# The product of two weights in a fused attention and two-MLP kernel: formed first in native float32 and kept in DRAM, instead of in the last block of the first MLP

## Chip, cores, metric

One core of one Trainium2 chip. The metric is the device time of one execution in microseconds; the kernel before takes 963.7 us (median of 3 runs).

## What is computed

```python
# attention: a recurrence over 768 steps, 4 batches x 8 heads of width 48
for t in range(S):
    S_re, S_im = ar*S_re - ai*S_im + k[t] v[t]^T, ar*S_im + ai*S_re
    y[t] = q[t] @ S_re
x = y as 3072 tokens x 384
# first MLP, d_ff = 2048
h = x @ w_in
g = max(h, 0) + log1p(exp(-abs(h)))
x = g @ w_out
# second MLP, d_ff = 1024; no nonlinearity between w3 and w_out
a = x @ w1;  b = x @ w2
h = a * b @ w3
return h @ w_out
```

The weights of both MLPs lie in DRAM as float64, which the kernel sees as pairs of int32 and turns into float32 itself.

## The kernel before

Tokens are 24 units of 128. Attention works unit by unit: a scan on DVE (`cmul`, tiles P and tm), a store and a transposing reload through DRAM (pd and rs), score matmuls (sc), DVE's mask (am), the matmuls yp, small DMAs that reorder y, and a copy to x. The first MLP (stage A) goes over nine blocks of tokens: 128, 256, then seven of 384. For each of 16 slices f of w_in and w_out (16 tiles of 128x768), `s1` multiplies by w_in and forms the softplus on ACT and DVE, and `s2a` adds the slice's share to three accumulators (acc); attention for later blocks is interleaved. The second MLP (stage B, `s3` and `s2b`) goes over six blocks of 512.

The first two blocks use native float32 matmuls with the weights w32; from the third on, weights and activations are split into a high and a low part of type float32r and multiplied in three products, each of which takes one pass.

Because nothing lies between w3 and the last w_out, the kernel forms their product W' (1024x384, tiles bwp) once and uses it in stage B. Before, this happens in the last block of stage A, in which no attention is left: `wo2_load` (L903) loads and converts eight pieces of w_out with three DVE operations (`to_f32`) and splits them; `w3_piece` (L913) does the same with 24 pieces of w3 transposed and issues three float32r matmuls per piece and column group into the PSUM tiles wpa; the last piece of a group splits the sums straight into bwp. `w12_conv` (L936) converts w1 and w2 in the same block. The loop at L949 sets when each is called.

wio (w_in and w_out of the first MLP) is converted in another, shorter way: `w_load` (L765) loads each half piece shifted by one int16, so that ACT's copy of bf16 to f16 (`wtop`) and one DVE operation give the float32 (`w_piece`, L774). These loads start at the beginning and go into eight buffers wb0 to wb7; the converted w32 lie in wa0 to wa15.

The order of all instructions is not the program's: `Plan` records every operation with a cost and a landing time from a table (`cost`, L128), simulates the engines (`run`, `flush`) and emits the best order found in 16 rounds. Every recorded operation therefore has one line in the profile, L200. SP issues all DMAs, in the planned order.

Of the kernel before, what the change touches and what calls it, by code (L numbers as in the profile page):

```python
# [11 lines left out]
F32 = mybir.dt.float32  # L12
F32R = mybir.dt.float32r
# [42 lines left out]
CV0 = 20  # L56
CVS = 10
LEAD = 0
ROUNDS = 16
SEED = 214  # L60
NBA = NT // NB
# [15 lines left out]
class Plan:  # L77
# [50 lines left out]
    def cost(self, eng, op, outs, ins):  # L128
        n = max(self.free_size(x) for x in (*outs, *ins))
        if eng == "SP":  # L130
            size = 2 if outs[0].dtype == I16 else 4
            for _, n in outs[0].ap:
                size *= n
            cost = max(650 if n < 512 and self.on_chip(ins[0]) else 475, size / 270)
            if not self.on_chip(outs[0]):
                land = 5200
            elif self.on_chip(ins[0]):
                land = 2300
            elif hasattr(ins[0].tensor, "tag_meta"):
                land = 6800  # L140
            else:
                land = 2500 + size / 270
            return cost, max(land - cost, 0)
        if eng == "PE":
            n = self.free_size(outs[0])
            if op == "transpose":
                return 109, 250
            m = outs[0].ap[0][1]
            if ins[0].dtype == F32R:
                return n / 2.4 + 14, 250  # L150
            return (0.75 * n + 24 if m <= 64 else max(n, m) / 0.6 + 5), 250
        if eng == "DVE":
            far = [x for x in ins if x.ap[-1][0] >= 4 and x.ap[-1][1] > 1]
            return 72 + n / (1.92 if op == "tensor_scalar" else 0.52 if len(far) > 1 else 0.95), 200
        if eng == "ACT":
            return 105 + 0.88 * n, 200
        return 160 + n * 2.08, 200
# [198 lines left out]
def fused(ctx: ExitStack, tc: tile.TileContext, a_in, qk_in, v_in, wio, w12, w3t, wo2, q, k, v, a_re, a_im, outT):  # L356
# [67 lines left out]
    def load(u):  # L424
        s = c[u]
        if u in (2, 3):
            t = sp.tile([P, KC, NB], F32, tag="xl", bufs=XB, name=f"a{u}")
            s["a"] = t.rearrange("p k n -> p (k n)")[:, 0 : 2 * GT].rearrange("p (c n) -> p c n", c=2)
        else:
            s["a"] = ap.tile([P, 2, GT], F32, tag="n2" if u == 1 else "a", bufs=1, name=f"a{u}")  # L430
        SP.dma_start(s["a"], a_in[u])
# [311 lines left out]
    def split(dst_h, dst_l, src):  # L743
        A.copy(dst_h, src)
        V.tensor_tensor(out=dst_l, in0=src, in1=dst_h.bitcast(F32), op=ALU.subtract)

    def to_f32(dst, raw):
        lo, hi, d = raw[:, :, 0], raw[:, :, 1], dst.bitcast(I32)
        V.tensor_scalar(
            out=d, in0=hi, scalar1=3, scalar2=0x3FFFFFF8, op0=ALU.logical_shift_left, op1=ALU.bitwise_and  # L750
        )
        V.scalar_tensor_tensor(
            out=d, in0=hi, scalar=-0x40000000, in1=d, op0=ALU.bitwise_and, op1=ALU.bitwise_or
        )
        V.scalar_tensor_tensor(
            out=d, in0=lo, scalar=29, in1=d, op0=ALU.logical_shift_right, op1=ALU.bitwise_or
        )
# [4 lines left out]
    for x in wtop:  # L762
        GP.memset(x, 0)

    def w_load(f):  # L765
        r = wraw[f] = wp.tile([P, 2 * DM, 2], I32, tag=f"wb{f % (FA // 2)}", name=f"wr{f}")
        n = 4 * DM
        for i in range(2):
            SP.dma_start(
                r.rearrange("p n w -> p (n w)").bitcast(I16)[:, i * n : (i + 1) * n - i],  # L770
                wio[f].bitcast(I16)[:, i * n + 1 : (i + 1) * n + 1 - i],
            )

    def w_piece(f):  # L774
        w32[f] = wp.tile([P, 2 * DM], F32, tag=f"wa{f}", name=f"w32_{f}")
        r, top = wraw.pop(f), wtop[f % 2 if f < FA - 1 else 0]
        A.copy(
            top.bitcast(F16).rearrange("p (n w) -> p n w", w=2)[:, :, 1],
            r.rearrange("p n w -> p (n w)").bitcast(BF16).rearrange("p (n w) -> p n w", w=4)[:, :, 2],
        )  # L780
        V.scalar_tensor_tensor(
            out=w32[f].bitcast(I32), in0=r[:, :, 0], scalar=13, in1=top, op0=ALU.logical_shift_right, op1=ALU.bitwise_or
        )

    whp = {}

# [78 lines left out]
            SP.dma_start(dst(i), o[:, 0:n])  # L865

    load(0)
    for f in range(4):
        w_load(f)
    first = att_end[BLOCKS[0][1] // T - 1]  # L870
# [6 lines left out]
    bwp = [None] * (FB // 2)  # L877
    bst = {}

    nraw, nwt, nw3 = count(), count(), count()  # L880

    def wt(name):
        tag, n = (("n2", 2 * DM), ("tm", 4 * TML))[next(nwt) % 2]
        return ap.tile([P, n], F32, tag=tag, name=name)[:, 0 : 2 * DM]

    def w3t_pair(name):
        i = next(nw3) % 3
        if i == 0:
            t = ap.tile([P, H * (64 + D)], F32R, tag="kT", name=name)
            return t[:, 0:DM], t[:, DM : 2 * DM]  # L890
        tags = ((("am", AMB, 4 * T), ("y", YB, 4 * T)), (("S", 2, DM),) * 2)[i - 1]
        return tuple(
            ap.tile([P, n], F32R, tag=tag, bufs=bufs, name=f"{name}_{j}")[:, 0:DM]
            for j, (tag, bufs, n) in enumerate(tags)
        )

    def raw3(src, n, name):
        tag, bufs = (("a", 1), ("qk", QB), ("nt", NTB))[next(nraw) % 3]
        r = ap.tile([P, DM, 2], I32, tag=tag, bufs=bufs, name=name)
        SP.dma_start(r[:, 0:n], src.rearrange("p (n w) -> p n w", w=2))  # L900
        return r[:, 0:n]

    def wo2_load(k):  # L903
        t = wt(f"wo2t{k}")[:, 0:DM]
        to_f32(t, raw3(wo2[k], DM, f"wo2r{k}"))
        if k % 2 == 0:
            tag, bufs, n = (("P", PB, 2 * R * GT), ("P", PB, 2 * R * GT), ("qkp", QKB, 4 * DM), ("rs0", 1, 2 * H * T))[k // 2]
            oo = ap.tile([P, n], F32R, tag=tag, bufs=bufs, name=f"wo2_{k}")
            bst["oo"] = oo[:, 0 : 4 * DM].rearrange("p (a b n) -> p a b n", a=2, b=2)
        o = bst["o", k] = bst["oo"][:, k % 2]  # L910
        split(o[:, 0], o[:, 1], t)

    def w3_piece(m0, n, k):  # L913
        t = wt(f"w3t{m0}_{k}")[:, 0 : n * P]
        to_f32(t, raw3(w3t[k, :, 2 * m0 * P : 2 * (m0 + n) * P], n * P, f"w3r{m0}_{k}"))
        w = w3t_pair(f"w3_{m0}_{k}")
        split(w[0][:, 0 : n * P], w[1][:, 0 : n * P], t)
        if k == 0:
            for i in range(n):
                bst["a", i] = pst(ATAG, ATT, [P, DM], f"wpa{m0 + i}")  # L920
        o = bst["o", k]
        for q, (a, b) in enumerate(((0, 0), (1, 0), (0, 1))):
            for i in range(n):
                PE.matmul(
                    bst["a", i], w[a][:, i * P : (i + 1) * P], o[:, b],
                    start=(k == 0 and q == 0), stop=(k == FB - 1 and q == 2),
                )
        if k == FB - 1:
            for i in range(n):
                m = m0 + i  # L930
                if m % 2 == 0:
                    bwp[m // 2] = w_tiles(m // 2, f"bwp{m // 2}")
                dh, dl = (x[:, (m % 2) * DM : (m % 2 + 1) * DM] for x in bwp[m // 2])
                split(dh, dl, bst["a", i])

    def w12_conv(j):  # L936
        t = wt(f"w12t{j}")
# [4 lines left out]
        split(bw[j][0], bw[j][1], t)  # L942

    nblk = len(BLOCKS)
    st = [lambda k=k: wo2_load(k) for k in range(FB)]
    for m0 in range(0, FB, 3):
        st += [lambda m0=m0, k=k: w3_piece(m0, min(3, FB - m0), k) for k in range(FB)]
    pos = 0
    for bi in range(nblk):  # L949
        last = bi == nblk - 1  # L950
        t0, n = BLOCKS[bi]
        if not last:
            start = att_pos[0]
            goal = att_end[sum(BLOCKS[bi + 1]) // T - 1] + LEAD
        gq = {}
        for f in range(FA):
            if bi == 0:
                if f + 4 < FA:
                    w_load(f + 4)
                if f + 2 < FA:  # L960
                    w_piece(f + 2)
            gq[f] = s1(bi, f)
            if f >= 2:
                s2a(bi, f - 2, gq.pop(f - 2))
            if not last:
                att_to(start + (goal - start) * (f + 1) // FA)
            elif f >= 2:
                while pos < len(st) * (f + 1) // FA:
                    st[pos]()
                    pos += 1  # L970
                if f >= 7 and f - 7 < FB - 2:
                    w12_conv(f - 7)
        for f in (FA - 2, FA - 1):
            s2a(bi, f, gq.pop(f))
        evac(n, lambda i: x2d[t0 // NB][:, i, t0 % NB : t0 % NB + n], f"a{bi}",
             lambda name: sp.tile([P, NB], F32, tag="e", name=name))
# [337 lines left out]
```

## Time and profile before

| | us |
|---|---|
| runs | 962.29, 963.7, 965.88 |
| median | 963.7 |
| the profiled execution's own time | 962.8 |
| its span | 961.0 |

The profile shows that one execution. Windows give the busy time of each engine in a stretch; a matmul's end is modelled, so neighbouring matmuls overlap, and the pace of PE is read from start to start. PEclk is the granted clock of TensorE as a share of full speed. The chain of waits is followed back from the last instruction.

### The profile page before, as it was taken

To read this page: it belongs to the slowest core of one execution; us is meant where nothing else is said; L and a number is where in the kernel's file an instruction comes from. 1 tells how busy PE (TensorE), PEld (TensorE's weight loads), DVE (VectorE), ACT (ScalarE), POOL (GpSimd) and SP (SyncE) were. 2 spreads that over 40 slices of the span, in tenths; PEclk is the share of its full clock that TensorE was granted. 3 is DMA by queue.
4 is the path that set the end of the run, shared out by engine and by line. 5 is a ranking of instruction groups with operands and counts; after the bars stand their busy time and mean duration, and the time that the engine had idled before them with its cause. 6 is when DMAs were issued, how large, how long until landed. Compare 5 with 4: busy or idle time off the path is not lost.

```text
span 961.0 us, 15859 instructions
## 1 busy us (share of the span) xinstructions
PE 876.4 (91%) x5737; PEld 807.5 (84%) x5737; DVE 769.4 (80%) x1707; ACT 539.3 (56%) x1108; POOL 6.8 (1%) x15
## 2 busy tenths in 40 slices
PE   0037899999999999999999999999999999999996
PEld 0027888899899999999999999998888888888885
DVE  7997999999998999999988787998978887422121
ACT  6766666686678786887775675564231322131221
POOL 2000000000000000000000000000000000000000
PEclk9997999999999999999999999999999999999998
DMA  8774563837365545446371844556877767100001
GB/s 322 293 178 127 124 158 85 196 92 142 98 143 128 126 111 134 118 101 180 87 158 64 194 161 154 165 156 189 247 244 244 258 200 243 45 33 1 34 0 37
DMA packets 87399, 138.61 MB, mean 144 GB/s; under 512 B 8080, under 2 KB 58384, under 8 KB 87312
## 3 DMA queue, kind: packets, MB, share of 16 engines
q1 hardware_dynamic: 87312, 137.52, 51.8%
q8 instruction: 46, 0.75, 0.4%
q14 instruction: 41, 0.34, 0.1%
HBM read 108.00 MB, written 28.31 MB: 142 GB/s over the span
## 4 chain that ended last, share of the span: by engine, by line
PE 80%; DVE 10%; DMA 6%; issue 1%; ACT 1%; SPq 1%; DVEq 0%; ACTq 0%
PE acc L200 29%; PE s L200 18%; PE pb L200 10%; PE pa L200 10%; PE wpa L200 3%; PE yp L200 3%; PE sc L200 3%; DVE P L200 3%; DMA a<-a_in 3%; DMA wr<-wio 2%; DVE tm L200 2%; PE stp L200 1%; DVE qkp L200 1%; SPq L200 1%; DMA rs<-pd 1%
## 5 line engine op out<-in xcount | busy, mean ns | idle before, releaser
L200 DVE TENSOR_TENSOR tm<-P 128x90 f32<-128x90 f32 (+3 forms) x240 | 145.8, 616 | 1.4
L200 ACT ACTIVATE e<-e 128x384 f32<-128x384 f32 (+2 forms) x288 | 135.4, 487 | 2.8
L200 DVE TENSOR_TENSOR bg<-pa,bg 128x512 f32<-128x512 f32 x48 | 33.0, 690 | 87.3 <-PE pa L200 70.9
L200 ACT ACTIVATE e<-s 128x384 f32<-128x384 f32 (+2 forms) x144 | 64.6, 452 | 48.5 <-PE s L200 40.1
L200 DVE TENSOR_TENSOR P<-tm 128x45 f32<-128x45 f32 (+11 forms) x304 | 86.1, 344 | 1.4
L200 DVE SCALAR_TENSOR_TENSOR g<-s,e 128x384 f32<-128x384 f32 (+2 forms) x144 | 73.8, 515 | 14.3 <-ACT e L200 12.0
L200 ACT CAST bgg<-bg 128x512 fp32r<-128x512 f32 x48 | 29.8, 621 | 98.1 <-DVE bg L200 98.1
L200 PE MATMUL ktp<-ident,qkp 128*128 128x128 f32 x120 | 21.4, 288 | 62.4 <-DVE qkp L200 60.2
L200 ACT COPY bg<-pb 128x512 f32<-128x512 f32 x48 | 28.2, 587 | 87.1 <-PE pb L200 87.1
L200 PEld LDWEIGHTS ktp<-ident,qkp 128*128 128x128 f32 x120 | 16.0, 149 | 63.8 <-issue 53.6
L200 ACT CAST gh<-g 128x384 fp32r<-128x384 f32 x112 | 56.6, 510 | 18.6 <-DVE g L200 16.2
L200 DVE TENSOR_TENSOR gl<-g,gh 128x384 fp32r<-128x384 f32 x112 | 62.2, 558 | 5.5 <-ACT gh L200 5.0
L200 PE MATMUL sc<-rs 112*128 112x128 f32 x384 | 56.7, 290 | 8.4 <-DMA rs<-pd 7.2
L200 PEld LDWEIGHTS sc<-rs 112*128 112x128 f32 x384 | 54.4, 204 | 9.5 <-issue 7.8
L200 DVE CUSTOM_DVE_ANT_0 ck<-ckr 128x384 f32<-128x384 f32 x80 | 43.4, 543 | 14.2 <-DMA ckr<-w3t 4.4
L200 PE MATMUL acc<-bgg,bwp0h 128*128 128x512 f32 x144 | 49.9, 389 | 0.0
L200 PE MATMUL acc<-bgg,bwp2h 128*128 128x512 f32 x144 | 47.7, 389 | 0.0
L200 DVE TENSOR_TENSOR bgg<-bg,bgg 128x512 fp32r<-128x512 f32 x48 | 32.9, 688 | 16.0 <-ACT bgg L200 15.9
L200 DVE TENSOR_REDUCE lims<-ck 128x1 f32<-128x384 f32 x80 | 43.0, 538 | 2.2
L200 PE MATMUL wpa<-wo,w 128*128 128x384 f32 x192 | 40.9, 335 | 0.0
L200 PE MATMUL s<-x,w 128*128 128x128 f32 (+1 forms) x192 | 38.0, 338 | 2.8 <-DVE g L200 2.2
L200 PE MATMUL yp<-am,v 128*48 128x128 f32 x384 | 36.3, 277 | 1.7 <-DVE am L200 1.7
(373 smaller groups left out, 2396.1 us busy)
## 6 DMA issues: line engine op xcount, KB each, us to landing
pd<-qkp SPq DMA_DIRECT2D x24, 768.0 KB, 4.4
rs<-pd SPq DMA_DIRECT2D x48, 384.0 KB, 5.9
ckr<-wio SPq DMA_DIRECT2D x32, 384.0 KB, 3.7
a<-a_in SPq DMA_DIRECT2D x24, 384.0 KB, 4.4
qk<-qk_in SPq DMA_DIRECT2D x24, 384.0 KB, 3.5
wr<-wio SPq DMA_DIRECT2D x16, 384.0 KB, 7.4
w3r<-w3t SPq DMA_DIRECT2D x16, 384.0 KB, 3.8
w12r<-w SPq DMA_DIRECT2D x16, 384.0 KB, 3.3
```

The lines of the kernel that those rows point to most:

```text
L200: getattr(engine.unit, op)(*args, **kw)
```

## The change

The product is formed by a new function, `early()`, called right after the first load of the attention's input and before all loads of wio. It loads w_out's last weight in four tiles of two pieces each (wor, wo) and w3 in groups of three, three and two columns of 128 (w3r, w), all shifted by one int16 and converted in the short way, which is now a function of its own (`convert`), and multiplies them as native float32, 64 matmuls of 128x384. The buffers are those of wio: wb0 to wb3 for wor, wb4 to wb7 for w3r, wa8 to wa11 for wo, wa12 to wa14 for w. ACT copies the sums out of PSUM, and SP stores them in a new DRAM tensor, wpd. In the last block of stage A, `wp_load` loads a pair of rows of W' and splits it. `wo2_load` and `w3_piece` are gone, as are their temporary tiles. In the table, a load from an input tensor costs size / 340 in place of size / 270 ns. Line numbers shift by two (L200 becomes L202).

```diff
+RATE = 340
...
-            cost = max(650 if n < 512 and self.on_chip(ins[0]) else 475, size / 270)
+            rate = 270 if hasattr(ins[0].tensor, "tag_meta") else RATE
+            cost = max(650 if n < 512 and self.on_chip(ins[0]) else 475, size / rate)
...
-                land = 2500 + size / 270
+                land = 2500 + size / rate
...
+    wpd = dram.tile([FB // 2, P, 2 * DM], F32, name="wpd", tag="wpd")
+
+    def early():
+        wo = []
+        pieces = []
+        for k in range(0, FB, 2):
+            r = wp.tile([P, 2 * DM, 2], I32, tag=f"wb{k // 2}", name=f"wor{k}")
+            for i in range(2):
+                shifted(r[:, i * DM : (i + 1) * DM], wo2[k + i])
+            wo.append(r)
+        for m0 in range(0, FB, 3):
+            n = min(3, FB - m0) * P
+            for k in range(0, FB, 2):
+                r = wp.tile([P, 2 * DM, 2], I32, tag=f"wb{4 + len(pieces) % 4}", name=f"w3r{m0}_{k}")[:, 0 : 2 * n]
+                for i in range(2):
+                    shifted(r[:, i * n : (i + 1) * n], w3t[k + i, :, 2 * m0 * P : 2 * (m0 * P + n)])
...
+                convert(w, r, next(ntop) % 2)
...
+                for h in range(2):
+                    for i in range(n // P):
+                        PE.matmul(
+                            o[i][:, 0:DM], w[:, h * n + i * P : h * n + (i + 1) * P], wo[k // 2][:, h * DM : (h + 1) * DM],
+                            start=(k + h == 0), stop=(k + h == FB - 1),
+                        )
+            for i in range(n // P):
+                m = m0 + i
+                e = sp.tile([P, NB], F32, tag="e", name=f"wpe{m}")
+                A.copy(e, o[i][:, 0:DM])
+                SP.dma_start(wpd[m // 2][:, (m % 2) * DM : (m % 2 + 1) * DM], e)
...
     load(0)
+    early()
     for f in range(4):
         w_load(f)
...
-    def wo2_load(k):
...
-    def w3_piece(m0, n, k):
...
+    def wp_load(i):
+        tag, bufs = (("a", 1), ("qk", QB), ("nt", NTB))[next(nraw) % 3]
+        r = ap.tile([P, 2 * DM], F32, tag=tag, bufs=bufs, name=f"wpr{i}")
+        SP.dma_start(r, wpd[i])
+        bwp[i] = w_tiles(i, f"bwp{i}")
+        split(bwp[i][0], bwp[i][1], r)
...
-            elif f >= 2:
-                while pos < len(st) * (f + 1) // FA:
-                    st[pos]()
-                    pos += 1
+            else:
+                if f >= 6 and f % 2 == 0 and f < 14:
+                    wp_load((f - 6) // 2)
```

How the planner orders the beginning, in three places. The first is SP's queue at the start of the program (a: attention's inputs; wor and w3r: the raw weights of the product; wr: raw pieces of wio). Before:

```order
L200 DMA a_138<-a_in 128x768
L200 DMA a_145<-a_in 128x768
L200 DMA a_147<-a_in 128x768
L200 DMA qk_165<-qk_in 128x768
L200 DMA a_157<-a_in 128x768
L200 DMA wr_140<-wio 128x1536
L200 DMA wr_139<-wio 128x1536
L200 DMA wr_139<-wio 128x1535
L200 DMA wr_140<-wio 128x1535
L200 DMA v_174<-v_in 128x384
```

Now:

```order
L202 DMA a_139<-a_in 128x768
L202 DMA wor_140<-wo 128x1535
L202 DMA a_194<-a_in 128x768
L202 DMA wor_140<-wo 128x1535
L202 DMA wor_141<-wo 128x1535
L202 DMA w3r_0_144<-w3t 128x1535
L202 DMA wor_141<-wo 128x1535
L202 DMA w3r_0_144<-w3t 128x1535
L202 DMA wor_142<-wo 128x1535
L202 DMA w3r_2_150<-w3t 128x1535 x2
```

Three of the first five loads of the attention's inputs are behind product weights now, and the first load of wio is the queue's 34th row. The second place is the same queue around the store of unit 0's qkp and its reload as rs. Before:

```order
L200 DMA wr_280<-wio 128x1535
L200 DMA wr_288<-wio 128x1535
L200 DMA wr_297<-wio 128x1535
L200 DMA qk_179<-qk_in 128x768
L200 DMA pd_65<-qkp_171 128x6x256
L200 DMA wr_297<-wio 128x1536
L200 DMA rs_130<-pd_65 48x8x256 x2
```

Now:

```order
L202 DMA pd_65<-qkp_220 128x6x256
L202 DMA v_223<-v_in 128x384
L202 DMA wr_191<-wio 128x1535 x2
L202 DMA wr_254<-wio 128x1535
L202 DMA wpd<-wpe_186 128x384
L202 DMA wpd<-wpe_187 128x384
L202 DMA rs_130<-pd_65 48x8x256 x2
```

Two stores of the product's last tiles (wpd) stand ahead of the reload of rs. The third place is DVE, in the scan of the first two units (tm and P; w and wo: conversions). Before:

```order
L200 TENSOR_TENSOR tm<-P_144 128x1536
L200 SCALAR_TENSOR_TENSOR w_0_156<-wr_139,wtop_ws 128x768
L200 TENSOR_TENSOR P_144<-tm 128x384 x2
L200 TENSOR_TENSOR P_152<-nt_149,P_152 128x3x128
L200 TENSOR_TENSOR tm<-P_144 128x768
L200 SCALAR_TENSOR_TENSOR P_152<-P_152,nt_149 128x3x128
L200 TENSOR_TENSOR P_144<-tm 128x192 x2
L200 SCALAR_TENSOR_TENSOR w_1_173<-wr_140,wtop_wa_137 128x768
L200 TENSOR_TENSOR tm<-P_144 128x384
```

Now:

```order
L202 TENSOR_TENSOR P_193<-a_194,nt_195 128x6x128
L202 SCALAR_TENSOR_TENSOR w_0_2_152<-w3r_2_150,wtop_wa_137 128x768
L202 TENSOR_TENSOR tm<-P_193 128x1536
L202 SCALAR_TENSOR_TENSOR wo_154<-wor_142,wtop_ws 128x768
L202 TENSOR_TENSOR P_193<-tm 128x384 x2
L202 TENSOR_TENSOR tm<-P_193 128x768
L202 SCALAR_TENSOR_TENSOR w_0_4_155<-w3r_4_153,wtop_wa_137 128x768
L202 SCALAR_TENSOR_TENSOR wo_157<-wor_143,wtop_ws 128x768
L202 TENSOR_TENSOR P_193<-tm 128x192 x2
L202 SCALAR_TENSOR_TENSOR w_0_6_158<-w3r_6_156,wtop_wa_137 128x768
```

The conversions between the scan's steps are those of the product's weights; ahead of unit 0's masked scores (am) there are 20 conversions, of which four belong to wio, where there were all 16 of wio and one split.

## Rows read from the trace of the kernel before

**Rows 1.** Page, part 1: busy time, share, instructions of each engine.

```profile
PE 876.4 (91%) x5737; PEld 807.5 (84%) x5737; DVE 769.4 (80%) x1707; ACT 539.3 (56%) x1108; POOL 6.8 (1%) x15
```

**Rows 2.** Stretches of 24 us: length, each engine busy (instructions), PEclk, DMA share, GB/s.

```profile
0.00:24.00 24.00, 0.00 (x0) 0.00 (x0) 17.03 (x31) 15.23 (x24) 6.78 (x15) 1.00 0.90 322
24.00:48.00 24.00, 0.00 (x0) 0.00 (x0) 23.66 (x56) 18.17 (x25) 0.00 (x0) 1.00 0.76 293
48.00:72.00 24.00, 8.11 (x59) 6.96 (x60) 23.76 (x56) 15.93 (x24) 0.00 (x0) 1.00 0.73 178
72.00:96.00 24.00, 18.00 (x174) 16.84 (x171) 18.99 (x37) 14.35 (x39) 0.00 (x0) 0.79 0.50 127
96.00:120.00 24.00, 20.90 (x224) 20.52 (x223) 22.94 (x66) 16.50 (x50) 0.00 (x0) 1.00 0.59 124
...
168.00:192.00 24.00, 22.61 (x127) 21.11 (x126) 24.00 (x60) 16.21 (x37) 0.00 (x0) 1.00 0.81 195
...
600.00:624.00 24.00, 24.00 (x140) 24.00 (x139) 22.25 (x47) 13.60 (x27) 0.00 (x0) 1.00 0.53 162
```

**Rows 3.** What PE waited for, 84 us to the end: us, times, longest.

```profile
PE sc L200 <- DMA rs<-pd: 3.1, 1, 3.1
PE s L200 <- DVE g L200: 2.5, 2, 2.2
PE ktp L200 <- DVE am L200: 2.2, 1, 2.2
```

**Rows 4.** The product's matmuls (tile wpa), and PE's timeline at 587 us: start, length.

```profile
L200 PE MATMUL wpa<-wo,w x192: 333/334/346, 584.0 to 667.8; 128*128 128x384 f32 x192
...
587.10 3.11 PE L200 MATMUL wpa<-wo,w 128*128 128x384 f32 x17
...
590.04 0.51 PE L200 MATMUL acc<-gh,ww0h 128*128 128x384 f32 x2
```

**Rows 5.** DVE groups, 540 to 675 us: busy us, mean ns, idle before.

```profile
L200 DVE SCALAR_TENSOR_TENSOR w3t<-w3r,w3t 128x384 int32<-128x384 int32 (+1 forms) x48 | 24.2, 511 | 0.5
...
L200 DVE TENSOR_SCALAR w3t<-w3r 128x384 int32<-128x384 int32 (+1 forms) x24 | 7.9, 335 | 1.4 <-DMA w3r<-w3t 1.3
```

**Rows 6.** Chain in order of time: native matmuls of 128 and 256 columns.

```profile
98.83 1.12 PE s L200 x10
...
154.79 2.59 PE acc L200 x12
```

**Rows 7.** Sixteen score matmuls, early (timeline) and later (chain), and both stretches.

```profile
65.28 3.59 PE L200 MATMUL sc<-rs 112*128 112x128 f32 x16 [2.07 <-DMA rs<-pd]
...
159.54 1.79 PE sc L200 x16
...
64.00:68.00 4.00, 2.72 (x13) 2.75 (x14) 3.93 (x13) 1.53 (x3) 0.00 (x0) 1.00 0.73 257
...
160.00:168.00 8.00, 8.00 (x66) 6.97 (x66) 8.00 (x17) 6.50 (x15) 0.00 (x0) 1.00 0.20 50
```

**Rows 8.** Timeline of the beginning: start us, length us, engine, operation.

```profile
12.51 1.03 ACT L200 CAST wtop_ws<-wr 128x768 f16<-128x768 bf16 x1
...
43.34 0.95 DVE L200 SCALAR_TENSOR_TENSOR w<-wr,wtop_wa 128x768 int32<-128x768 int32 x1
44.21 1.02 DVE L200 TENSOR_TENSOR P<-tm 128x381 f32<-128x381 f32 x2
...
76.72 5.06 SPq L200 DMA_DIRECT2D y<-y  x6
...
83.05 0.51 ACT L200 COPY x<-y 128x384 f32<-128x384 f32 x1 [2.42 <-DMA y<-y]
...
83.62 2.27 PE L200 MATMUL s<-x,w 128*128 128x128 f32 x18
```

**Rows 9.** A stretch with the DMA queue full, and the loads of rs (timeline).

```profile
36.00:40.00 4.00, 0.00 (x0) 0.00 (x0) 3.90 (x9) 2.01 (x4) 0.00 (x0) 1.00 1.04 403
...
57.83 0.84 SPq L200 DMA_DIRECT2D rs<-pd  x2
```

More of the change, by code (lines that the diff above doesn't have):

```diff
@@ L763, in fused, with shifted, convert @@
         GP.memset(x, 0)
+    def shifted(dst, src):
+        n = 2 * dst.shape[1]
+        SP.dma_start(dst.rearrange("p n w -> p (n w)").bitcast(I16)[:, 0 : 2 * n - 1], src.bitcast(I16)[:, 1 : 2 * n])
     def w_load(f):
         r = wraw[f] = wp.tile([P, 2 * DM, 2], I32, tag=f"wb{f % (FA // 2)}", name=f"wr{f}")
-        n = 4 * DM
         for i in range(2):
[L769 to L776, printed above, removed]
+            shifted(r[:, i * DM : (i + 1) * DM], wio[f, :, 2 * i * DM : 2 * (i + 1) * DM])
+    ntop = count()
+    def convert(dst, r, which):
+        n = r.shape[1]
+        top = wtop[which][:, 0:n]
         A.copy(
@@ L781, in w_piece @@
         V.scalar_tensor_tensor(
-            out=w32[f].bitcast(I32), in0=r[:, :, 0], scalar=13, in1=top, op0=ALU.logical_shift_right, op1=ALU.bitwise_or
+            out=dst.bitcast(I32), in0=r[:, :, 0], scalar=13, in1=top, op0=ALU.logical_shift_right, op1=ALU.bitwise_or
         )
+    def w_piece(f):
+        w32[f] = wp.tile([P, 2 * DM], F32, tag=f"wa{f}", name=f"w32_{f}")
+        convert(w32[f], wraw.pop(f), f % 2 if f < FA - 1 else 0)
+    wpd = dram.tile([FB // 2, P, 2 * DM], F32, name="wpd", tag="wpd")
@@ new lines, in early @@
+    def early():
[12 more added lines that the diff above has]
+                    shifted(r[:, i * n : (i + 1) * n], w3t[k + i, :, 2 * m0 * P : 2 * (m0 * P + n)])
+                j = len(pieces)
+                if m0 == 0:
+                    t = wp.tile([P, 2 * DM], F32, tag=f"wa{8 + k // 2}", name=f"wo{k}")
+                    convert(t, wo[k // 2], next(ntop) % 2)
+                    wo[k // 2] = t
+                w = wp.tile([P, 2 * DM], F32, tag=f"wa{12 + j % 3}", name=f"w3_{m0}_{k}")[:, 0 : 2 * n]
+                convert(w, r, next(ntop) % 2)
+                pieces.append(w)
+                if k == 0:
+                    o = [
+                        pst(f"acc{i}", 1, [P, NX], f"wpa{m0 + i}") if m0 != 3 else pst("s1", S1B, [P, NX], f"wpa{m0 + i}")
+                        for i in range(n // P)
+                    ]
+                for h in range(2):
[9 more added lines that the diff above has]
+                SP.dma_start(wpd[m // 2][:, (m % 2) * DM : (m % 2 + 1) * DM], e)
@@ L878, in fused @@
     bst = {}
-    nraw, nwt, nw3 = count(), count(), count()
+    nraw, nwt = count(), count()
     def wt(name):
@@ L884, in wt @@
         return ap.tile([P, n], F32, tag=tag, name=name)[:, 0 : 2 * DM]
[L886 to L895, printed above, removed]
     def raw3(src, n, name):
@@ L901, in raw3 @@
         return r[:, 0:n]
-    def wo2_load(k):
[L904 to L911, printed above, removed]
-    def w3_piece(m0, n, k):
[L914 to L934, printed above, removed]
+    def wp_load(i):
[4 more added lines that the diff above has]
+        split(bwp[i][0], bwp[i][1], r)
     def w12_conv(j):
@@ L944, in fused @@
     nblk = len(BLOCKS)
[L945 to L948, printed above, removed]
     for bi in range(nblk):
```

## The prediction

> **What bounds the kernel now.** I read the stretches first. From about 96 us on the windows show PE busy all the time or nearly so, up to the last block [rows 2]; DVE is as full up to 192 us, and over the whole span it stands at 769.4 us of 961 against 876.4 us for PE [rows 1]. The list of what PE waited for after 84 us adds up to 10.0 us, of which the three longest entries make up 7.8 us [rows 3]. So from the first block's first matmul on (83.6 us, [rows 8]) PE has a list of work and works it off: what leaves this list shortens the kernel by its PE time, and a later start of the list lengthens it. Before 83.6 us PE is nearly empty: 0.00 us of work in the first 48 us and 8.11 us in the next 24 [rows 2]. There DVE sets the pace, 23.66 and 23.76 us of 24. The change moves work from the full part into the empty one, through the engine that is full there.
>
> **Part 1: what leaves the end.** The product now takes 192 fp32r matmuls between 584 and 668 us [rows 4]. Their durations (334 ns) overlap, so I count start to start: 17 in a row from 587.10 us, the next matmul at 590.04, are 2.94/17 = 0.173 us each. 192 x 0.173 = **33.3 us** of PE time, in windows where PE is busy 24.00 of 24 [rows 2]. I count all of it. What could be late next there is DVE: it loses the conversions of w3t and wo2 (48 of 0.511 and 24 of 0.335 us for w3t alone, 32 us, [rows 5]) and gets four loads of the finished product with one cast and one subtraction each, so it is emptier than before. The conversions of w1 and w2 stay there.
>
> **Part 2: what PE gets at the start.** 64 native float32 matmuls of 128x384; the trace writes a native one as two instructions, and has none of 384 columns. Start to start, an instruction takes 1.12/10 = 0.112 us at 128 columns and 2.59/12 = 0.216 us at 256 [rows 6], a step of 0.104 us, so I estimate 0.32 us at 384: 128 x 0.32 = **41 us** at the full rate. The lower bound is 128 x 0.216 = 28 us, the upper one twice 41. PE was idle for that long before, so I count 0 for it, as long as it ends before the attention needs PE. The first pieces are loaded and converted at about 14 us (the first conversion's cast ran at 12.51 us before, [rows 8]); 14 + 41 = 55 us, and the score matmuls that lead to the first x started at 65.28.
> PE's rate at the start is the uncertain point. [...] I allow one piece at half rate, 3.9 us, inside the slack: at half rate PE has more work than DVE brings it (six matmuls of a piece are 7.7 us, and in the new order 3 to 4 us of DVE work lie between two pieces of w3t), so it works without a gap from the second piece on.
>
> **Part 3: what the loads get.** 24 transfers of 384 KB and 8 of 256 KB, 11.5 MB, go ahead of the 32 wio transfers (12.6 MB). The queue moved 403 GB/s when full [rows 9], so that is 29 us. Until 72 us 19 MB moved before [rows 2] (322, 293 and 178 GB/s for 24 us each); with 11.5 MB more and 1.6 MB of stores it is 32 MB, 80 us at that rate. The last wio piece is then ready just when block 0 starts, not well before. On SP the unit's load of rs now stands behind the last two stores of the product, each of which waits for an ACT copy and that for PE: at 14 + 41 + 3.9 + 1 = 60 us, against 57.83 [rows 9].
>
> **Part 4: what DVE and ACT get.** 16 conversions more, of 0.87 us from start to start (43.34 to 44.21, [rows 8]), four of them only 512 wide (about 0.6): 12.8 us on the engine that is full, and 16 casts plus 8 copies on ACT, which has room (15 to 18 us of 24). But the order puts 12 of the 16 wio conversions behind unit 0's attention: ahead of unit 0's masked scores stand 20 conversions (16 x 0.87 + 4 x 0.6 = 16.3 us) where 16 and one split of the same size stood (14.8), 1.5 us more. With the 2 us of SP I take **+3 us** for the first x; bounds 0 and 12.8 (all sixteen in its way). The other 12 x 0.87 = 10.4 us fall behind it, where DVE was idle for 5.0 us in 72 to 96 and 1.1 us in 96 to 120, and was full in 168 to 192 [rows 2]. Between 10.4 - 6.1 = 4.3 us (all that idle time taken up) and 10.4 us is what PE then waits for x in blocks 1 and 2; I take **+7 us**, in the middle; the lower bound is 0, if PE has old blocks to work on.
>
> **Part 5: the table.** 340 in place of 270 B/ns only changes what the planner believes of input loads. No instruction is added by it. A better order can't gain more than the 10.0 us that PE waited after 84 us [rows 3]; I take 0.
>
> **Sum.** The profiled execution took 962.8 us: 962.8 - 33.3 + 3 + 7 = 939.5. The median of the runs, 963.7, is 0.9 above it: **940**.
>
> **The rivals.**
> A (forecast): as summed, 940, own range 935 to 946. Chance 0.52.
> B, everything is hidden: the first x is on time, and the 12 late conversions fall into DVE's idle time or hold up only units whose x PE does not need yet. 962.8 - 33.3 + 0.9 = 930. For it: DVE's row order up to unit 0 is nearly even. Against it: DVE 24.00 of 24 in 168 to 192. Chance 0.16.
> C, the start is bound by DVE and the loads together: all sixteen conversions delay the first x, and the 12 late ones count in full: 962.8 - 33.3 + 12.8 + 10.4 + 0.9 = 954. For it: the queue has no gap until 80 us, and y's copies (76.72 to 83.05, [rows 8]) go through the same queue; a wait of SP on a store holds up every load behind it. Chance 0.18.
> D, slower than before: the product stays at PE's half rate. 128 x 0.64 = 82 us from 14 us on end at 96. The load of rs stands on SP behind the last stores of the product, so it is issued at 97 us in place of 57.83, and the first x is 39 us late: 962.8 - 33.3 + 39 + 7 + 0.9 = 976. It decides against the change once the first x is more than 33.3 - 7 = 26 us late, that is when two thirds of the product run at half rate. For it: the 3.59 us [rows 7], at the end of a stretch in which PE had almost nothing to do. Against it: pieces come faster than PE works them off. Chance 0.09. [...]
> E, the end doesn't shrink by what is removed: the last block waits for w12's conversions or for loads, and only half of the 33.3 us comes: 962.8 - 16.6 + 10 + 0.9 = 957. Against it: DVE's work there falls by more than 32 us. Chance 0.05.
>
> **How the numbers follow.** The likeliest case gives 940. The range from 928 to 955 takes in A, B and C and leaves out D and E, 0.14, and a little at the ends. About 0.5% (4.8 us) is what a measurement of this kernel can tell from no change. Faster by more than that means under 958.9: A, B, C and part of E, 0.88; within 0.5%: the rest of E and the edge of C and D, 0.04; slower: most of D, 0.08.
>
> **What would show it.** In the profile after: wpa matmuls from about 14 to 58 us, of about 0.32 us from start to start after the first few; PE's first block matmul at 84 to 89 us (A), 83 (B), 95 or later (C), above 115 (D); in 84 to 192 us more idle time of PE than before, with DVE as the releaser; 16 more us of DVE work before 120 us; and a last block of about 50 us in place of 84, with PE still without gaps. The forecast is wrong if PE waits in the last block, if the first x is later than 95 us, or if PE's waits after the first block matmul grow by more than 13 us.

## The result, and the profile after

The changed kernel takes 948.25 us (median of 4 runs, 946.74 to 949.90) against 963.54 us (4 runs); the ratio is 0.9839, interval 0.9814 to 0.9864. That is 15.3 us less, inside the predicted range of 928 to 955 and 8.3 us above the predicted 940. The profiled execution of after took 949.9 us, its span is 948.2 us. In every run below, the span of the profiled execution lies 1 to 2 us under its time. The two profiled executions are 12.8 us apart in span, so an account of the profiles has 12.8 us to explain and not 15.3.

The page's first part, which answers to [rows 1]:

```profile
PE 889.4 (94%) x5673; PEld 800.3 (84%) x5673; DVE 729.9 (77%) x1591; ACT 538.5 (57%) x1096; POOL 6.8 (1%) x15
```

The stretches of [rows 2], with the same columns:

```profile
0.00:24.00 24.00, 9.66 (x26) 5.66 (x27) 16.04 (x23) 15.11 (x21) 6.78 (x15) 1.00 0.91 343
24.00:48.00 24.00, 24.00 (x76) 14.20 (x75) 21.61 (x56) 13.39 (x22) 0.00 (x0) 1.00 0.99 329
48.00:72.00 24.00, 14.13 (x53) 9.55 (x53) 23.83 (x48) 14.42 (x27) 0.00 (x0) 0.78 0.94 282
72.00:96.00 24.00, 17.43 (x146) 16.57 (x145) 22.02 (x53) 17.02 (x39) 0.00 (x0) 0.72 0.94 280
96.00:120.00 24.00, 18.45 (x176) 17.84 (x175) 20.98 (x45) 20.67 (x49) 0.00 (x0) 0.86 0.85 235
120.00:144.00 24.00, 18.49 (x152) 16.63 (x152) 19.79 (x45) 21.11 (x48) 0.00 (x0) 0.86 0.64 178
```

The product fills PE from 14 to 58 us as forecast. What was not forecast stands in the last three lines: between 72 and 144 us PE is busy 54.4 us (62.9 in the same three stretches of before), the DMA share from 72 to 120 us is 0.94 and 0.85 where it was 0.50 and 0.59, ACT works 58.8 us where it did 47.3, and the granted clock is 0.72, 0.86 and 0.86 (0.79, 1.00 and 0.93 in before). The third of these stretches in before:

```profile
120.00:144.00 24.00, 24.00 (x171) 21.45 (x170) 22.84 (x49) 16.42 (x41) 0.00 (x0) 0.93 0.64 156
```

The beginning on the timeline (start, length, engine, operation), the places of [rows 8] and [rows 9]:

```profile
14.34 41.05 PE L202 MATMUL wpa<-wo,w 128*128 128x384 f32 x122 [14.34 <-DVE w L202]
...
55.88 2.10 PE L202 MATMUL wpa<-wo,w 128*128 128x384 f32 x6
...
60.51 0.93 SPq L202 DMA_DIRECT2D rs<-pd  x2
...
85.68 5.39 PE L202 MATMUL s<-x,w 128*128 128x128 f32 x32 [2.65 <-ACT x L202]
```

An instruction of the product takes 41.05/122 = 0.336 us on average, and the last ends at 58.0 us. The load of rs is issued 2.7 us later than before, and the first matmul of block 0 starts 2.1 us later.

What PE waited for from 85 us to the end, against [rows 3]:

```profile
PE s L202 <- ACT x L202: 8.2, 2, 5.5
PE s L202 <- ACT xh L202: 6.3, 4, 4.0
PE s L202 <- DVE w L202: 3.5, 1, 3.5
PE s L202 <- DVE g L202: 2.0, 1, 2.0
PE acc L202 <- ACT bgg L202: 1.7, 2, 1.3
```

The largest are waits for x and xh, the attention's result for the next block. The whole list adds up to 23.4 us, against 10.0 in before.

The span can be taken apart into three terms: it is the start of the first block matmul, plus PE's busy time from there on, plus PE's idle time from there on. The lines are one stretch each, from that matmul to the end (length, PE busy, ...), of before and of after:

```profile
83.62:961.00 877.38, 859.87 (x5581) 792.86 (x5581) 695.73 (x1548) 484.15 (x1026) 0.00 (x0) 0.99 0.50 135
```

```profile
85.68:948.20 862.52, 834.47 (x5453) 764.43 (x5453) 656.76 (x1437) 486.54 (x1014) 0.00 (x0) 0.99 0.49 134
```

The start moves by +2.1, the busy time by -25.4 and the idle time by +10.5 (17.5 to 28.1 us): -12.8 in all. The 33.3 us that left the end aren't all seen in the busy time: 8 us came back as busy time of PE, and 10.5 as idle time. Most of both arises before block 2, whose first matmul starts at 194.5 us instead of 178.9. Of the 8 us, 2.8 are work that only changed its place: the matmuls yp and stp of unit 1, 64 instructions, ran from 79.36 to 83.6 us in before, ahead of block 0, and run from 105.19 to 108.0 us in after, inside it (5453 instructions behind the first block matmul, where 5581 - 192 = 5389 are left of before).

### The profile page after: what moved, and what is told of

Same layout as the page of the kernel before. It is cut to its first block, busy times and chain, and to the rows that moved or that the text cites. A ratio compares the mean times of both kernels' runs of the same rounds, so it can differ in the third digit from the quotient of the medians.

```text
span 948.2 us, 15624 instructions
## 1 busy us (share of the span) xinstructions
PE 889.4 (94%) x5673; PEld 800.3 (84%) x5673; DVE 729.9 (77%) x1591; ACT 538.5 (57%) x1096; POOL 6.8 (1%) x15
## 4 chain that ended last, share of the span: by engine, by line
PE 69%; DMA 13%; DVE 11%; ACT 3%; issue 3%; SPq 1%; DVEq 0%; ACTq 0%
PE acc L202 25%; PE s L202 20%; PE pa L202 6%; PE pb L202 6%; PE sc L202 4%; PE yp L202 3%; DMA ckr<-w3t 3%; DMA ckr<-wio 3%; DMA wr<-wio 3%; DVE ck L202 2%; PE wpa L202 2%; DMA pd<-qkp 2%; DVE P L202 2%; PE stp L202 1%; DVE tm L202 1%
## 5 line engine op out<-in xcount | busy, mean ns | idle before, releaser
L202 DVE TENSOR_TENSOR tm<-P 128x90 f32<-128x90 f32 (+3 forms) x240 | 144.6, 616 | 1.5
L202 ACT ACTIVATE e<-e 128x384 f32<-128x384 f32 (+2 forms) x288 | 135.8, 487 | 2.7
L202 DVE TENSOR_TENSOR bg<-pa,bg 128x512 f32<-128x512 f32 x48 | 33.0, 688 | 91.8 <-PE pa L202 81.5
L202 ACT ACTIVATE e<-s 128x384 f32<-128x384 f32 (+2 forms) x144 | 64.6, 451 | 54.0 <-PE s L202 50.8
L202 ACT CAST bgg<-bg 128x512 fp32r<-128x512 f32 x48 | 29.8, 621 | 114.7 <-DVE bg L202 114.7
L202 DVE SCALAR_TENSOR_TENSOR g<-s,e 128x384 f32<-128x384 f32 (+2 forms) x144 | 73.6, 515 | 24.5 <-ACT e L202 24.4
L202 DVE TENSOR_TENSOR P<-tm 128x45 f32<-128x45 f32 (+11 forms) x304 | 87.2, 344 | 1.6
L202 ACT COPY bg<-pb 128x512 f32<-128x512 f32 x48 | 28.2, 587 | 85.2 <-PE pb L202 78.4
L202 DVE TENSOR_TENSOR gl<-g,gh 128x384 fp32r<-128x384 f32 x112 | 62.1, 559 | 5.8 <-ACT gh L202 5.1
L202 ACT CAST gh<-g 128x384 fp32r<-128x384 f32 x112 | 56.7, 507 | 16.1 <-DVE g L202 11.5
L202 PE MATMUL sc<-rs 112*128 112x128 f32 x384 | 55.1, 286 | 7.3 <-DMA rs<-pd 7.3
L202 PEld LDWEIGHTS sc<-rs 112*128 112x128 f32 x384 | 53.2, 201 | 8.7 <-issue 7.8
L202 DVE CUSTOM_DVE_ANT_0 ck<-ckr 128x384 f32<-128x384 f32 x80 | 43.4, 542 | 21.6 <-DMA ckr<-w3t 9.7
L202 PE MATMUL wpa<-wo,w 128*128 128x384 f32 x128 | 43.2, 499 | 14.3 <-DVE w L202 14.3
L202 PE MATMUL s<-x,w 128*128 128x128 f32 (+1 forms) x192 | 40.8, 363 | 13.7 <-ACT x L202 8.2
L202 PE MATMUL acc<-bgg,bwp0h 128*128 128x512 f32 x144 | 50.8, 391 | 1.7 <-ACT bgg L202 1.3
L202 PEld LDWEIGHTS wpa<-wo,w 128*128 128x128 f32 x128 | 24.9, 196 | 31.5 <-DVE w L202 14.5
L202 PE MATMUL acc<-bgg,bwp2h 128*128 128x512 f32 x144 | 49.2, 392 | 1.2 <-DVE bgg L202 0.8
L202 PEld LDWEIGHTS s<-x,w 128*128 128x128 f32 x192 | 33.7, 218 | 17.5 <-ACT x L202 8.6
L202 DVE TENSOR_TENSOR bgg<-bg,bgg 128x512 fp32r<-128x512 f32 x48 | 33.0, 688 | 16.3 <-ACT bgg L202 16.3
L202 DVE TENSOR_REDUCE lims<-ck 128x1 f32<-128x384 f32 x80 | 43.1, 538 | 2.3
L202 PE MATMUL yp<-am,v 128*48 128x128 f32 x384 | 36.3, 279 | 2.0 <-ACT nt L202 2.0
```

The lines of the kernel that those rows point to most:

```text
L202: getattr(engine.unit, op)(*args, **kw)
```

## The experiments

Theory 1 was that ACT and DVE are full in blocks 0 and 1, because the conversions of wio and the casts of ww fell into them; theory 2, that the DMA queue brings wio too late. In five of the runs (ACT or DVE relieved alone, half of the loads, and the two that combine these) the order on every engine is that of after: the planner sees the instruction as it was, and an argument `real` replaces what is issued (`()`: nothing). The others are planned anew, so their times also hold what another order is worth; the run with the other seed, below, gives a measure of that, 3 to 5 us.

**The end alone.**

```diff
     load(0)
-    early()
...
-        SP.dma_start(r, wpd[i])
+        SP.dma_start(r, wo2[i].bitcast(F32))
```

> The product isn't formed; the last block loads four tiles of w_out's raw bits in place of the stored product and splits them, so the end of the kernel is the changed one and the beginning has no product in it. The profiles put 2.1 us of the shortfall at the first x, 13.6 us between it and the first matmul of block 2, and some 3 us behind block 2. If the cost is in the beginning (all theories of the next three runs), this gives 963.5 - 33.3 = 930, with the 3 us behind block 2 kept 933: 928 to 935. If instead the end gives back less than the 33.3 us of matmuls, 940 or more.

The product isn't formed, and the last block loads raw bits of w_out in its place. Measured: 929.61 us (ratio 0.9649, 0.9614 to 0.9684), 33.8 us less than before (963.37, measured beside it). Its line from the first block matmul on:

```profile
86.59:929.90 843.31, 826.19 (x5390) 757.15 (x5389) 639.76 (x1412) 469.42 (x985) 0.00 (x0) 0.99 0.47 129
```

PE's busy time falls by 859.87 - 826.19 = 33.7 us, idle time stays (17.1). So the end gives back all of the 33.3 us, and all that is missing, 948.25 - 929.61 = **18.6 us**, is the price of forming the product at the beginning, where the prediction had 10. Between the two profiles it is 18.3 us: the first block matmul 0.9 us earlier in after, PE's busy time from there on 8.3 us more, its idle time 10.9 us more. It has arisen by block 2, whose first matmul starts at 173.69 us in this run and at 194.47 in after, and most of it in block 0: from its first matmul to that of block 1 it takes 31.8 us here (86.59 to 118.34) and 46.9 in after (85.68 to 132.61).

**Fewer loads, and the engines relieved one at a time.**

```diff
-            r = wp.tile([P, 2 * DM, 2], I32, tag=f"wb{k // 2}", name=f"wor{k}")
+            r = wp.tile([P, 2 * DM, 2], I32, tag="wb0", name="wor") if k == 0 else r
...
-                r = wp.tile([P, 2 * DM, 2], I32, tag=f"wb{4 + len(pieces) % 4}", name=f"w3r{m0}_{k}")[:, 0 : 2 * n]
+                if not pieces:
+                    raw = wp.tile([P, 2 * DM, 2], I32, tag="wb4", name="w3r")
...
+                r = raw[:, 0 : 2 * n]
```

> The product's conversions and matmuls all run, but from one raw tile of w_out and one of w3 (2 of 16 loaded; the product is wrong): 10 MB of the 11.5 MB of loads ahead of wio are gone, and the planner makes its order anew. Theory 1 (ACT and DVE are full in blocks 0 and 1, because wio's casts, conversions and the casts of ww fell into them): the same instructions remain, so little comes back, 943 to 948. Theory 2 (the DMA queue: wio arrives too late, so its conversions have to fall there): with wio up to 25 us earlier most of the 13.6 us comes back, 933 to 939.

Measured: 942.12 us (0.9780, 0.9745 to 0.9815), 6.1 us less than after: between the ranges of the two theories, which both missed, and a third of the 18.6.

```diff
+            real=() if dst.tensor.name[:3] == "w32" else None,
...
-        split(ww[f][0], ww[f][1], w32[f])
+        A.copy(ww[f][0], w32[f], real=())
+        V.tensor_tensor(out=ww[f][1], in0=w32[f], in1=ww[f][0].bitcast(F32), op=ALU.subtract, real={"in1": w32[f]})
...
+                    real=(o, alt(w, k), xx[:, k, 0:n]),
```

> Same order on every engine as the changed kernel; left out are ACT's 16 casts of wio and 16 casts that make the high half of ww (the matmuls take one constant tile in place of the high half), some 26 instructions or 24 us of ACT behind the first x. Theory 1 with ACT as the engine that counts: 8 to 13 us come back, 935 to 940. With DVE as the engine that counts (the prediction's term of 7 us), or theory 2: under 3 us, 945 to 948.

(`alt` puts a constant tile in the place of the high halves.) Measured: 948.34 us (0.9834, 0.9794 to 0.9874). Nothing came back from ACT in this order, although its busy time over the first 216 us fell from 149.0 to 125.7 us. My first reading of the profile after, that the casts on ACT by themselves hold x back, falls.

```diff
-            out=dst.bitcast(I32), in0=r[:, :, 0], scalar=13, in1=top, op0=ALU.logical_shift_right, op1=ALU.bitwise_or
+            out=dst.bitcast(I32), in0=r[:, :, 0], scalar=13, in1=top, op0=ALU.logical_shift_right, op1=ALU.bitwise_or,
+            real=(lambda: nc.gpsimd.tensor_copy(dst, r.rearrange("p n w -> p (n w)").bitcast(I16).rearrange("p (n w) -> p n w", w=4)[:, :, 0])) if dst.tensor.name[:4] == "w32_" else None,
```

(POOL copies every fourth int16 of the raw piece.)

> Same order on every engine; the 16 conversions of wio on DVE are copies on POOL, which is idle otherwise, so 12 x 0.87 = 10.4 us of DVE work behind the first x are gone and ACT keeps all of its work. DVE as the engine that counts: 6 to 10 us come back, 938 to 942. ACT as the engine that counts, or theory 2: under 3 us, 945 to 949.

Measured: 945.45 us (0.9818, 0.9782 to 0.9853): 2.8 us, and the interval overlaps that of after.

**Half of the loads, and all together, in the order of after.** First every second load of the product, with the first half of a raw tile read twice by the cast and the conversion:

```diff
-                shifted(r[:, i * DM : (i + 1) * DM], wo2[k + i])
+                shifted(r[:, i * DM : (i + 1) * DM], wo2[k + i], i == 1)
...
-                    shifted(r[:, i * n : (i + 1) * n], w3t[k + i, :, 2 * m0 * P : 2 * (m0 * P + n)])
+                    shifted(r[:, i * n : (i + 1) * n], w3t[k + i, :, 2 * m0 * P : 2 * (m0 * P + n)], i == 1)
...
-        SP.dma_start(dst.rearrange("p n w -> p (n w)").bitcast(I16)[:, 0 : 2 * n - 1], src.bitcast(I16)[:, 1 : 2 * n])
+        SP.dma_start(
+            dst.rearrange("p n w -> p (n w)").bitcast(I16)[:, 0 : 2 * n - 1], src.bitcast(I16)[:, 1 : 2 * n],
+            real=() if half else None,
+        )
```

> Same order on every engine; of the product's 32 loads every second one is left out, and the conversions use the first half of each tile twice (the product is wrong). 5.75 MB fewer stand ahead of wio, and every cast, conversion and matmul remains. Theory 2 (the queue: it is full until 120 us and moves 282, 280 and 235 GB/s from 48 to 120 us, not 403, so the last pieces of wio come when block 0 should be over): wio comes up to 5.75 MB / 0.28 = 20 us earlier, most of the 13.6 us goes, 936 to 942. Theory 1 (ACT and DVE work of wio fallen into blocks 0 and 1): 945 to 949.

Measured: 946.73 us (0.9836, 0.9811 to 0.9861).

Then the two edits of the ACT and the DVE run in one kernel:

> Same order; the edits of the two runs with one engine relieved taken together: no casts of wio, no casts for the high half of ww on ACT, and wio's conversions as copies on POOL instead of DVE. Loads are unchanged. Theory 1 in its last form (the two engines cover for each other, so one alone gives nothing): 936 to 942. Theory 2: as the better of the two alone, 943 to 948.

Measured: 947.61 us (0.9836, 0.9809 to 0.9863).

And these two edits with the one of the loads:

> Same order; both of the two runs before together. If loads and engines each hold a part of the 13.6 us, this gives less than either: 930 to 937. If the fixed order itself (unit 1's matmuls and v load placed behind block 0's on PE and SP) holds the time, it stays at 940 or above.

Measured: 949.95 us (0.9859, 0.9836 to 0.9881). (In both, PE waits for wio's pieces from POOL at one or two places, 1.3 and 3.2 us.)

With half of the product's loads, ACT's casts of wio and of the high halves and DVE's conversions of wio all gone, the time is what it was: the last sentence of that expectation holds. **The order itself carries the time**, and neither theory 1 nor theory 2 does without a new order. Two waits of PE show it best: before block 1 it waits 5.51 us for ACT's copy of x in after, and 5.51 or 5.52 us in each of the five runs in its order; before block 2 it waits 3.99 us for xh, and 3.96 to 4.04 in the five. Where short work stands behind long work in this order, SP's timeline of that last run shows by one example:

```profile
82.97 7.75 SPq L204 DMA_DIRECT2D wr<-wio  x11
95.01 0.38 SPq L204 DMA_DIRECT2D pd<-qkp  x1
95.44 0.53 SPq L204 DMA_DIRECT2D wr<-wio  x1
96.06 0.93 SPq L204 DMA_DIRECT2D v<-v_in  x1
```

SP issues eleven loads of wio, then stands until DVE has made qkp (94.03 us, 0.95 us long), and only then issues the v of unit 1. DVE had masked that unit's scores at 86.16 us; PE multiplies them with v at 104.85, behind a row of block 0's matmuls. PE comes to them straight from that row, without a wait, so in this list v is not what they wait for; and no run moves the v alone. That the place of v on SP costs time is thus not shown; that unit 1's attention stands behind block 0's matmuls is. The order of after does the same:

```profile
82.39 7.45 SPq L202 DMA_DIRECT2D wr<-wio  x11
96.02 0.38 SPq L202 DMA_DIRECT2D pd<-qkp  x1
96.45 0.54 SPq L202 DMA_DIRECT2D wr<-wio  x1
97.08 1.11 SPq L202 DMA_DIRECT2D v<-v_in  x1
```

and before had that v at 72.81 us and copied unit 1's x at 103.89; after copies it at 125.01. Block 1, of 256 tokens, needs units 1 and 2: it starts at 132.61 us (before 122.37), when ACT has copied unit 2's x (at 132.05; before 121.81), and block 2 follows at 194.5. Unit 2's last matmuls stand at the end of PE's list for block 0 (yp from 122.69 us), and behind them only 1.6 us of work are left for PE until their result is back as x. Removing work from DVE, ACT or the queue mostly lets the engines wait at the same places of their lists.

**Theory 3: the order comes from what the table says of the loads.** So I turned to the line of the change that the prediction had put at 0.

```diff
-RATE = 340
+RATE = 270
```

> The changed kernel with RATE back at 270, nothing else. The prediction's part 5 (the table only changes what the planner believes; 0): 945 to 951. Rival: with slower loads in its table the planner puts the attention of units 1 and 2 and wio's conversions still later, because it believes wio comes later, and blocks 0 and 1 grow again by several us: 953 or above.

Measured: 958.39 us (0.9947, 0.9928 to 0.9965). The rival holds: the table's new number is worth 10.1 us of the 15.3, and the product with the old table would have gained 4.6 us over before (963.0, measured beside it). SP issues the last load of wio at 120.6 us in this order (after: 104.4), unit 1's x is copied at 136.33 and block 1 starts at 147.00.

The kernel before, with the new table:

```diff
 LEAD = 0
+RATE = 340
...
-            cost = max(650 if n < 512 and self.on_chip(ins[0]) else 475, size / 270)
+            rate = 270 if hasattr(ins[0].tensor, "tag_meta") else RATE
+            cost = max(650 if n < 512 and self.on_chip(ins[0]) else 475, size / rate)
```

> The kernel before with the changed table (340) and nothing else. Theory 3 (the table counts only as far as it makes the planner put work behind late loads; before, wio is in by 60 us with either rate): no gain, 960 to 966. Rival (340 is simply nearer to the truth and helps any order of this program by the 10 us that it gave the changed kernel): 953 to 957.

Measured: 962.57 us against 961.57 (1.0005, 0.9992 to 1.0018): alone, the table does nothing. It is worth something in the changed program, where wio's loads come behind the product's.

And the other way, in the changed kernel:

```diff
-RATE = 340
+RATE = 450
```

> The changed kernel with RATE at 450, more than the queue has ever moved in a trace here (403 GB/s). Theory 3 (the order of blocks 0 and 1 holds the time, and that order comes from how late the planner believes wio to be): the attention of unit 1 moves ahead again, block 2 starts before 190 us, and the whole gains 4 to 10 us, 938 to 944. Theory 2 (the queue can't deliver sooner): the order believes in loads that don't come, PE, ACT and DVE wait for wr in it, 947 to 955.

Measured: 951.38 us (0.9880, 0.9855 to 0.9905), in the range of theory 2; theory 3 had forecast 938 to 944 and block 2 before 190 us, and it starts at 194.59. SP issues the last load of wio at 95.4 us, 9.0 earlier than in after, but the attention pays: the load of rs is issued at 66.89 instead of 60.51 and the first x copied at 94.06 instead of 85.11. So a faster table isn't better by itself. That 340 is the best number isn't shown: the 3 us between 340 and 450 are no more than the next run finds between two orders from one table.

```diff
-SEED = 214
+SEED = 9
```

> The changed kernel with another seed (9 in place of 214) for the planner's one noisy round: how much of all this is the luck of one order. If the order's luck is small beside 10 us, 943 to 950; with the first x of unit 1 as late as before (118 to 126 us), since that doesn't come from the noise.

Measured: 951.21 us (0.9894, 0.9871 to 0.9917), a little above the expected range, unit 1's x at 124.81 us. Another order from the same table is 3 us off (5 by the ratios, 0.9894 against 0.9839), against 10 for the table, and unit 1 is as late in it. So the 10.1 us of the table and the late unit 1 are hardly luck, as far as one other seed can tell; differences of 3 to 5 us between runs that are planned anew could be.

**Both limits lifted, and a new order.** Theory 4 was that the loads and the product's 16 conversions on DVE each hold the order back. The edit is made in the run with one piece of each weight, in the conversion, behind ACT's cast:

```diff
+        if dst.tensor.name[:3] != "w32":
+            raw16 = r.rearrange("p n w -> p (n w)").bitcast(I16).rearrange("p (n w) -> p n w", w=4)
+            GP.tensor_copy(dst, raw16[:, :, 0])
+            return
```

> The run with one piece of each weight (10 MB of loads less, planned anew, 942.1), and in it the product's 16 conversions on DVE as copies on POOL, which was idle (the product is wrong; casts, matmuls, copies and stores of the product remain), again planned anew. Theory 4 (loads and DVE's conversions are two limits of the same stretch, and either one alone holds the order back; the rest of the product is free): the whole cost of the beginning goes, 963.5 - 33.3 = 930, and block 2 starts before 180 us: 928 to 935. Rival (matmuls, casts and copies of the product on PE and ACT, or PE's lower clock in the gaps, cost time of their own): 938 to 943, as without the edit.

Measured: 938.35 us (0.9762, 0.9742 to 0.9782), 3.8 us less than with fewer loads alone, though the intervals of the two ratios overlap and another order could make as much: at the edge of the rival's range, not in theory 4's. Block 2 starts at 188.46 us, not before 180. The same account as above, for the runs that carry the argument (start of the first block matmul, PE busy and idle from there on, span, all from one stretch of each trace):

| run | first matmul | busy | idle | span |
|---|---|---|---|---|
| before | 83.6 | 859.9 | 17.5 | 961.0 |
| after | 85.7 | 834.5 | 28.1 | 948.2 |
| the end alone | 86.6 | 826.2 | 17.1 | 929.9 |
| table 270 | 91.1 | 838.0 | 28.2 | 957.2 |
| one piece | 89.4 | 830.6 | 20.3 | 940.3 |
| one piece, POOL | 90.6 | 825.5 | 20.5 | 936.6 |

With neither loads nor DVE's conversions in the way, the busy time is that of the end alone and the idle time 3.3 us above it; what is left is mainly a first matmul 4.0 us later. In this run the product itself ends later, at 64.0 us: before its last 14 instructions PE waits 5.12 us for DVE's qkp, which attention's ktp needs (POOL's last copy had ended at 49.4 us):

```profile
11.96 39.50 PE L202 MATMUL wpa<-wo,w 128*128 128x384 f32 x114 [11.96 <-POOL w L202]
56.58 1.54 PE L202 MATMUL ktp<-ident,qkp 128*128 128x128 f32 x6 [5.12 <-DVE qkp L202]
57.91 6.06 PE L202 MATMUL wpa<-wo,w 128*128 128x384 f32 x14
```

Of the 18.6 us at the beginning, 6.1 went in the run without most of the loads and 3.8 more in the one without DVE's conversions, both with some us for the luck of an order; 938.35 - 929.61 = 8.7 stay with the product's matmuls, casts, copies and stores, or with POOL as a stand-in. These weren't taken apart: that is open. Of the runs with the whole computation (both tables, the other seed) none was faster than the changed kernel.

## Why the prediction came out as it did

**Part 1 (-33.3) was right**: -33.8 in the time, -33.7 in PE's busy time. Rival E (the end doesn't shrink) falls. One small loss at the end stays untested: from 584 us on, PE is idle 10.7 us in after (364.2 us, 353.5 busy), 7.9 in the run of the end alone (345.9, 338.05) and 7.3 in before (377.0, 369.69).

**Part 2 was right in its times**: 0.336 us an instruction on average (estimate 0.32, with 3.9 us more allowed for a first piece at half rate), product over at 58.0 us (58 or 59). No run shows that term of 3.9 us: in after the first four of the piece's twelve instructions stand 0.64 to 0.80 us from start to start, the fifth 0.43, and all others of the row 0.32, so the slow start cost about 1.5 us. So rival D had no place. Its price of 0 is not shown: the open 8.7 us contain it.

**Part 3 failed**, in the step "The queue moved 403 GB/s when full", which set the last piece of wio to the start of block 0. With the DMA share at 0.94 the queue moved 282 and 280 GB/s, and 235 in the next stretch, at 0.85; the last load of wio was issued at 104.4 us, 19 us after block 0 had begun. One window of wide loads [rows 9] was taken as the rate of a mixture that has stores, reloads and y's small copies in it (what each of these costs wasn't measured). The windows of after add up to 29.6 MB by 96 us and so to the 32 MB of that part at about 106 us, not 80. But the rate isn't the whole of it: with half of the product's loads left out, in the same order, the last load of wio still goes out at 101.7 us, and with all of them, in the order of the table at 450, at 95.4. The planned order holds these loads back as well.

**Part 4**: the first x was right (+2.1, forecast +3). The term of +7 measured 13.6: from the first block matmul to that of block 2 it took 95.2 us before (83.6 to 178.85) and 108.8 after (85.7 to 194.47). The reason given, DVE's twelve late conversions, is not it by itself: taking wio's conversions off DVE in the same order gave 2.8 us. DVE wasn't the full engine there either: in 96 to 144 us it was busy 40.8 of 48 us, and up to 120 us it had 104.5 us of work where before had 106.4, not 16 us more; PE's longest waits ended with ACT (x and xh, 14.5 of the 23.4 us), and not with DVE. What the term did not look at is the place of unit 1's attention in the new order, behind block 0's matmuls.

**Part 5 failed**, in the step "No instruction is added by it ... I take 0". The bound was taken from the kernel before, where PE waited 10.0 us; but the table acts on the new program, in which wio comes late. There it is worth 10.1 us, about the whole bound. With the old table, the beginning costs 958.39 - 929.61 = 28.8 us.

So the forecast's sum for the beginning, 3 + 7 + 0 = 10, stands against 28.8 - 10.1 = 18.6: two terms were too small in size and of opposite sign, and that they cancel in part is luck: with the old table the same forecast would have met 958.39, outside its range. One of its own signs of being wrong also appeared: PE's waits after the first block matmul were to grow by at most 13 us, and the list grew by 13.4 (10.0 to 23.4 us; the idle time grew by 10.5). Rival C, "bound by DVE and the loads together", named the right pair but priced it by adding conversions; the run with both lifted gives 9.9 us to the pair, planned anew, and the other 8.7 us are open.

## What to carry to other kernels

Moving work into the idle time of one engine can cost time through the stretch's other resources and through the order (here 18.6 of the 33.8 us); count the queue at the rate of the mixture that it carries there (282 and 280 GB/s), not at its best window (403). In a kernel whose order is planned from a table, test the table's entries and the move apart: a number that does nothing before the move may decide after it. Measure with several seeds what another order alone is worth, before a difference of a few us is given a cause. And when relieving every engine in a fixed order changes nothing, the order is the bottleneck: look for waits that stay the same in all these runs, and for the work that stands ahead of what they wait for.

## What the runs showed of the hardware

In after, the granted clock falls in blocks 0 and 1 too (0.86 from 96 to 144 us); the forecast allowed half rate only at the start. After the two longest waits of PE there, 3.55 and 5.51 us, the next matmuls are slower than the same ones later on, and the granted clock is lower. Timeline of PE in after:

```profile
100.53 0.94 PE L202 MATMUL s<-x,w 128*128 128x128 f32 x6 [2.00 <-DVE g L202]
...
114.05 1.62 PE L202 MATMUL s<-x,w 128*128 128x128 f32 x6 [3.55 <-DVE w L202]
...
121.38 0.83 PE L202 MATMUL s<-x,w 128*128 128x128 f32 x6
...
132.61 7.90 PE L202 MATMUL s<-x,w 128*128 128x256 f32 x26 [5.51 <-ACT x L202]
...
143.44 2.32 PE L202 MATMUL s<-x,w 128*128 128x256 f32 x10
```

and stretches of 4 us:

```profile
112.00:116.00 4.00, 1.95 (x9) 1.98 (x10) 2.68 (x9) 3.93 (x9) 0.00 (x0) 0.61 0.77 285
116.00:120.00 4.00, 4.00 (x22) 4.00 (x22) 4.00 (x6) 3.50 (x9) 0.00 (x0) 0.54 0.18 56
...
132.00:136.00 4.00, 3.39 (x8) 2.77 (x9) 3.96 (x8) 3.08 (x6) 0.00 (x0) 0.50 0.86 158
136.00:140.00 4.00, 4.00 (x18) 3.44 (x18) 2.83 (x5) 3.34 (x10) 0.00 (x0) 0.91 0.64 203
```

Six matmuls take 1.62 us after a wait of 3.55 us, with the clock at 0.61 and 0.54 in the two stretches from 112 us, and 0.83 us later on. After the wait of 5.51 us the clock stands at 0.50, and 26 matmuls take 7.90 us, 0.30 us each, where ten at 143.44 us take 2.32, 0.23 us each. These two waits of PE thus cost more than their length; the one of 2.00 us did not, six matmuls took 0.94 us behind it. How long a wait has to be for that was not measured. The run with the end alone shows a granted clock of 1.00 from its first block matmul to 140 us, where after shows 0.84. Of the 8.3 us of busy time between the two, 2.8 are unit 1's matmuls inside block 0; the other 5.5 fall on as many instructions in both runs, which take longer in after. That fits the lower clock, whose share was not measured by itself.

The product in native float32 isn't cheaper for PE than the one that it replaces: 128 instructions, two for each of the 64 matmuls, from 14.3 to 58.0 us, 43.6 us (0.65 of them six other matmuls; the first four instructions 0.64 to 0.80 us from start to start, from 17.5 us on 0.32), against 192 x 0.173 = 33.3, one instruction for each float32r matmul. The gain is one of place alone.
